# First batch's main keys turned with all 128 rows, a PSUM bank per head, and identity products in TensorE's planned gaps there

## The chip, the cores and the metric

One core of a Trainium2 chip. The metric is the device time of one execution in microseconds; a profiled execution has its own time, and its span runs from the first to the last instruction.

## The reference

Three layers, all in fp32, on 4 batches, 8 heads, 576 positions, head size 64. Attention: q and k are rotated by position, `scores = q·k / 8`, a softmax over the keys, then times v. The heads are put side by side to 512 columns. The first moe block mixes each position with the one before (`mu_k`, `mu_r`), computes `k = relu(xk @ w_k)`, `v = k*k @ w_v`, `r = sigmoid(xr @ w_r)`, and gives `r * v`. The second computes `h = relu(x @ w_in)`, normalises its second half over the columns, mixes it over the positions with `w_spatial`, multiplies it with the first half, and applies `w_out`.

## The kernel before, in words

The kernel has two halves. In the first one, attention for the batches runs beside the first moe block; in the second, the rest runs batch by batch. The change touches only the first half.

There the work is cut in 72 units of attention (`unit`, from line 305): 18 per batch, each 128 queries of a pair of heads; the last 64 queries of two neighbouring pairs make one unit together, the tail (every ninth unit has `tail` set). A unit does, in this order of need: `scores` (line 315; the first batch, `i < EXACT`, in plain fp32 with 64 rows for each head, line 338; later batches as three fp32r products, lines 327 and 330); `top`, the row maximum, on VectorE (line 342); `expo`, the exponential with its row sum, on ScalarE, one for each head (line 347); `total`, `norm` and `spread`, which make 1/sum and copy it to 64 columns (lines 351, 354, 358); `turn(0)` and `turn(1)`, which turn the probabilities so that the keys lie on the partitions (line 367); `turn_rest` for the last 64 keys and the spread sums (lines 377, 380, 381); `take(0)`, `take(1)` on ScalarE and `take_rest` on VectorE, which copy the turned blocks from PSUM to SBUF (lines 395, 400, 402); and for every second unit `values`, the product with v, (line 409) and `gather`, which scales it and writes it into the moe input (line 421).

`turn(n)` issues eight transposes: for each of four blocks of 128 keys of head n, two of 64 rows (queries 0 to 63 and 64 to 127). The result `t` has two PSUM banks, one for each half of the queries, so that each copy (`take`, four of the eight blocks of both banks) reads both banks.

`feed` (from line 461) holds the first moe block of a batch, `mk` (line 505) and `mv` (line 544), which runs beside the next batch's attention. `prep` (from line 236) loads and rotates q and k on VectorE (lines 249, 257), and `weight64` prepares weights on VectorE, ScalarE and GpSimd (lines 142 to 174). The identity `ident` is written once by GpSimd (lines 222 and 225).

All of this is put in order by a planner (`Plan`, lines 51 to 101). Each step has an engine, a planned duration, the steps it needs, a rank, and a slot that it takes or gives back. `order` plays the plan through: of the steps that are ready, an engine takes the one of least rank; TensorE takes one that is ready first, and pays `SWITCH` where the kind of its steps changes. The slots are PSUM banks: two `m` banks (values, remaining turns, moe), one `t` (the two banks of the turns). The steps are then emitted sorted by their planned beginning, and each engine runs its own in that order; the framework adds the waits. The planned costs that matter here: `turn` 0.27 us, `expo` 0.93, `top` 0.75, `take` 0.59.

Of the kernel before, what the change touches and what calls it, by code (L numbers as in the profile page):

```python
# [7 lines left out]
F32 = mybir.dt.float32  # L8
# [17 lines left out]
EXACT = NP  # L26
WB, GB, WB2, GB2 = 3, 2, 3, 2
RAW, ROT, VB, PFB, PTB, XTS = 2, 4, 2, 3, 2, 6
KB, RLB, VSB = 4, 2, 1
EARLY, EVERY = 24, 2.9  # L30
WAIT, SWITCH, BONUS = 0.3, 0.1, 0.0
SIDES = slice(0, HALF), slice(HALF, S)
HEAD = slice(0, 64), slice(64, 128)

# [16 lines left out]
class Plan:  # L51


    def __init__(self, room):
        self.steps, self.room = [], room

    def add(self, eng, us, fn, deps=(), rank=0.0, after=0.12, take=None, give=None, port=False, kind=None):
        s = Step(eng, us, fn, deps, rank, after, take, give, port, kind)
        self.steps.append(s)
        return s  # L60

    def order(self):
        free = dict.fromkeys(("PE", "ACT", "DVE", "POOL", "SP"), 0.0)
        room = {k: [(0.0, i) for i in range(n)] for k, n in self.room.items()}
        todo = {e: [s for s in self.steps if s.eng == e] for e in free}
        left, port, kind = len(self.steps), {"DVE": 0.0, "POOL": 0.0}, None
        while left:
            best = None
            for e, steps in todo.items():
                ready = []  # L70
                for s in steps:
                    if any(d.end is None for d in s.deps) or s.take and not room[s.take]:
                        continue
                    ready.append((max([free[e]] + [d.end + d.after for d in s.deps]
                                      + ([min(room[s.take])[0]] if s.take else [])
                                      + ([port["POOL" if e == "DVE" else "DVE"]] if s.port else [])), s))
                if ready:
                    soon = min(t for t, _ in ready) + (WAIT if e != "PE" else 0.0)
                    t, s = min((x for x in ready if x[0] <= soon), key=lambda x: (x[1].rank - (BONUS if e == "PE" and x[1].kind == kind else 0.0), x[0]))
                    if best is None or t < best[0]:  # L80
                        best = t, s
            t, s = best
            s.begin, s.end = t, t + s.us
            if s.eng == "PE" and s.kind != kind:
                kind = s.kind
                s.end += SWITCH
            free[s.eng] = s.end
            if s.port:
                port[s.eng] = s.end
            if s.take:  # L90
                s.slot = min(room[s.take])[1]
                room[s.take].remove(min(room[s.take]))
            if s.give:
                room[s.give.take].append((s.end + s.after, s.give.slot))
            todo[s.eng].remove(s)
            left -= 1
        return sorted(self.steps, key=lambda s: s.begin)

    def emit(self):
        for s in self.order():  # L100
# [4 lines left out]
def body(ctx: ExitStack, tc, qp, kp, vp, cs, mu_k, mu_r, w_k, w_v, w_r, w_in, w_sp, b_sp, w_out, out):  # L105
    nc = tc.nc
# [8 lines left out]
    ps_m = ph1p.enter_context(tc.tile_pool(name="ps_m", bufs=1, space=PSUM))  # L115
# [3 lines left out]
    ps_t = att.enter_context(tc.tile_pool(name="ps_t", bufs=1, space=PSUM, side="right"))  # L119
# [4 lines left out]
    v_dram = [dram.tile([128, 4, S], F32, tag=f"vd{b}", name=f"vd{b}") for b in range(B)]  # L124

    cst = at.tile([128, 2, S], F32, name="cst")
    ends = [[at.tile([128, 128], F32R, tag=f"qe{i}{k}", name=f"qe{i}{k}") for k in range(2)] for i in range(2)]
    ident = const.tile([128, 128], F32, name="ident")
    mix4 = const.tile([128, NP, 4], F32, name="mix4")
# [72 lines left out]
    wv = [wpool.tile([128, NFC, DM], F32R, tag=f"wB{i}", name=f"wv{i}") for i in range(2)]  # L202

    second, fed = {}, set()
    plan = Plan({"m": 2, "e": 4, "t": 1, "ww": WB, "wg": GB})
    add = plan.add

    def which(m):
# [3 lines left out]
    ropes, vloads, exps, turned, valued, xdone, stored = {}, {}, {}, {}, {}, {}, {}  # L212
# [92 lines left out]
    def unit(m):  # L305
        w = which(m)
        tail = len(w) == 2
        st = units[m] = {}
        g, k = divmod(m, 9)
        part = 0 if tail else (k - (k > 4)) % 2  # L310
# [49 lines left out]
        def turn(n, slot=None):  # L360

            if n == 0:
                st["t"] = ps_t.tile([128, 2, 8, 64], F32, tag="t", name=f"t{m}")
            for c in range(4):
                for h, r in enumerate(HEAD):
                    k = 64 * (h if tail else n) + 128 * c
                    nc.tensor.transpose(st["t"][:, h, 4 * n + c, :], st["p"][r, n, k:k + 128], ident[r, r])  # L367

        def turn_rest(slot):

            pt, p = ps_m.tile([128, 4, 128], F32, tag=f"m{slot}", name=f"u{m}"), st["p"]
            st["u"] = pt
            if tail:
                for u in range(2):
                    for k in range(2):
                        for j, r in enumerate(HEAD):
                            nc.tensor.matmul(pt[r, u, HEAD[k]], st["r"][r, u, :] if k else p[r, u, 512 - 512 * j:576 - 512 * j],  # L377
                                             ident[r, r], start=True, stop=True)
            else:
                nc.tensor.transpose(pt[:, 0, :], p.rearrange("p a b -> p (a b)")[:, 512:640], ident)  # L380
                nc.tensor.transpose(pt[:, 1, :], st["r"].rearrange("p a b -> p (a b)"), ident)

        def turned_to(u):
            d = into[u if tail else 0]
# [4 lines left out]
        def take(k):  # L389
            o = turned_to(k)  # L390
            if tail:
                o = o[:, 0:8, 256:320].rearrange("p (h c) q -> p h c q", h=2)
            else:
                o = o[:, 4 * k:4 * k + 4, 128 * part:128 * part + 128].rearrange("p c (h q) -> p h c q", h=2)
            nc.scalar.copy(o, st["t"][:, :, 4 * k:4 * k + 4, :])  # L395
# [39 lines left out]
        t = add("ACT", 0.2, total, [exps[m, 1]], m - 0.3)  # L435
        nm = add("DVE", 0.17, norm, [t], m - 0.3)
        sp = add("ACT", 0.26, spread, [nm], m - 0.3)
        late = [y for d in into for y in freed.get(d["n"] - PTB, [])]
        t = add("PE", 0.27, lambda slot: turn(0), [exps[m, 0]], m + -0.02, take="t", kind="s")
        turned[m, 0] = x = add("PE", 0.27, lambda: turn(1), [exps[m, 1], t], m + 0.05, kind="s")  # L440
        x = add("ACT", 0.59, lambda: take(1), [x] + late, m - 0.2, 0.05)
        x = add("ACT", 0.59, lambda: take(0), [x] + late, m - 0.2, give=t)
        turned[m, 1] = t = add("PE", 0.55 if tail else 0.22, turn_rest, [sp], m + 0.2, take="m", kind="t")
        y = add("DVE", 0.55 if tail else 0.42, take_rest, [t] + late, m - 0.2, give=t)
        for d in into:
            d["ev"] += [x, y]
        if part and k != 3 or tail:
            v = add("PE", 2.9 if duo["cols"] > 256 else 2.3, values, duo["ev"] + [vloads[w[0][0]]], m + 0.9, take="m", kind="v")
            i = w[0][0]
# [205 lines left out]
    for n, (k, c, q) in enumerate(todo):  # L655
        if k == "x":
            mix_steps(c, 76 + n, close)
        else:
            add("SP", 0.4, lambda k=k, c=c, q=q: nc.sync.dma_start(
                raw(second[k == "i"][:, :, c, DM * q:DM * q + DM]), w_dram[0 if k == "r" else 1 + q][:, c]), [close], 76 + n, 5)  # L660
    add("ACT", 1.3, opened, [close], 75)
    with tc.manual_schedule():
        plan.emit()

# [236 lines left out]
```

## Time and profile before

| | us |
|---|---|
| median of 3 runs | 772.25 |
| lowest, highest | 770.16, 772.73 |
| the profiled execution | 773.33 |
| its span | 771.5 |
| TensorE busy in the span | 723.5 |

Engines: PE is TensorE, PEld its weight loads, DVE is VectorE, ACT ScalarE, POOL GpSimd, SP SyncE. Busy shares of TensorE are of pipelined matmuls, whose ends are modelled. A plain fp32 matmul leaves two records. A granted clock of 1.00 is TensorE's full 2.4 GHz, 0.50 is 1.2 GHz.

### The profile page before, as it was taken

Reading aid. Unit: us, or ns where it says so; the run is one execution under the profiler, and the core shown is the slowest. Engines: PE = TensorE matmul, PEld = TensorE weight load, DVE = VectorE, ACT = ScalarE, POOL = GpSimd, SP = SyncE. Lnnn points to the kernel's source line nnn. Section 1 sums busy time; section 2 is a strip of 40 time slices with the busy share of each in tenths; the row PEclk is TensorE's granted clock in tenths of the full one; section 3 lists DMA queues with packets and bytes.
Section 4 is the critical chain, followed back from the end, with each engine's and each line's share of the span. In section 5 each row is a group of like instructions: output and inputs, shape, how many; then the busy total and the mean of one; then the engine's idle time right before and its main releaser. Section 6 shows DMA issues by size and latency. Waiting matters only on the chain.

```text
span 771.5 us, 15273 instructions
## 1 busy us (share of the span) xinstructions
PE 723.5 (94%) x6208; PEld 636.9 (83%) x6208; DVE 473.5 (61%) x881; ACT 456.4 (59%) x1045; POOL 112.5 (15%) x132
## 2 busy tenths in 40 slices
PE   3787779899999999999999999999999999999998
PEld 2554448698798788888798799989989999998997
DVE  5769898886886986886866444247363342545111
ACT  4667888887877887777887554246334332533211
POOL 2243245012002021022031000002020000101000
PEclk9989899999999999999999999999999999999999
DMA  8355432442543353443351085082201212010101
GB/s 296 117 158 167 132 116 79 149 122 87 177 132 135 119 173 107 134 143 105 119 174 63 16 297 192 25 264 83 62 1 63 63 47 78 17 31 1 62 1 62
DMA packets 35273, 84.20 MB, mean 109 GB/s; under 512 B 4545, under 2 KB 10433, under 8 KB 35202
## 3 DMA queue, kind: packets, MB, share of 16 engines
q1 hardware_dynamic: 34658, 82.63, 32.6%
q8 instruction: 49, 0.80, 0.4%
q10 hardware_dynamic: 544, 0.59, 0.3%
q14 instruction: 22, 0.18, 0.1%
HBM read 60.65 MB, written 22.55 MB: 108 GB/s over the span
## 4 chain that ended last, share of the span: by engine, by line
PE 87%; ACT 5%; DMA 4%; DVE 3%; issue 1%; SPq 1%; ACTq 0%; DVEq 0%
PE v L409 12%; PE mk L505 12%; PE mv L544 11%; PE sp L680 8%; PE r L680 7%; PE u L680 7%; PE hv L744 7%; PE o L680 7%; PE t L367 6%; PE s L330 5%; PE s L338 3%; ACT pt L395 3%; PE u L380 1%; PE s L327 1%; DMA I-6413_6414<-xd 1%; DMA wi<-wd 1%
## 5 line engine op out<-in xcount | busy, mean ns | idle before, releaser
L342 DVE TENSOR_REDUCE sm<-s 128x1 f32<-128x576 f32 x144 | 106.0, 750 | 28.4 <-PE s L330 20.3
L347 ACT ACTIVATE pf<-s,sm 128x576 f32<-128x576 f32 x144 | 106.6, 749 | 10.6 <-DVE sm L342 10.5
L505 PE MATMUL mk<-x,wk 128*128 128x288 f32 x768 | 110.8, 300 | 0.7 <-DVE pt L400 0.7
L544 PE MATMUL mv<-kh,wv 128*128 128x288 f32 x512 | 109.2, 299 | 0.9 <-DVE pt L402 0.5
L505 PEld LDWEIGHTS mk<-x,wk 128*128 128x128 f32 x768 | 104.0, 190 | 1.7 <-PE u L377 0.8
L395 ACT COPY pt<-t 128x512 f32<-128x512 f32 x144 | 77.6, 589 | 41.5 <-PE t L367 40.7
L409 PE MATMUL v<-pt,vt 128*64 128x256 f32 (+1 forms) x640 | 90.8, 433 | 8.5 <-ACT pt L395 8.2
L367 PEld LDWEIGHTS t<-ident,pf 64*128 64x128 f32 x1152 | 56.3, 141 | 47.0 <-ACT pf L347 22.6
L367 PE MATMUL t<-ident,pf 64*128 64x64 f32 x1152 | 68.8, 232 | 21.0 <-ACT pf L347 20.9
L544 PEld LDWEIGHTS mv<-kh,wv 128*128 128x128 f32 x512 | 83.8, 188 | 2.7 <-issue 1.2
L409 PEld LDWEIGHTS v<-pt,vt 128*64 128x64 f32 x640 | 45.7, 144 | 42.9 <-ACT pt L395 11.3
L544 PE MATMUL mv<-kl,wv 128*128 128x288 f32 x256 | 75.7, 296 | 0.4 <-DVE kl L523 0.4
L680 PE MATMUL sp<-ws,vn 128*128 128x288 f32 x384 | 53.9, 295 | 0.0
L680 PE MATMUL r<-xr,wr 128*128 128x288 f32 x384 | 52.5, 296 | 1.2 <-ACT vs L550 1.2
L680 PE MATMUL o<-g,wo 128*128 128x288 f32 x384 | 52.9, 296 | 0.5 <-ACT os L803 0.5
L680 PEld LDWEIGHTS r<-xr,wr 128*128 128x128 f32 x384 | 51.7, 188 | 1.8 <-ACT vs L550 1.5
L680 PEld LDWEIGHTS sp<-ws,vn 128*128 128x128 f32 x384 | 52.4, 188 | 0.7
L680 PEld LDWEIGHTS o<-g,wo 128*128 128x128 f32 x384 | 51.7, 188 | 1.4 <-ACT os L803 1.2
L680 PE MATMUL u<-x,wi 128*128 128x288 f32 x384 | 52.0, 296 | 0.0
L680 PEld LDWEIGHTS u<-x,wi 128*128 128x128 f32 x384 | 51.6, 188 | 0.3
L249 DVE TENSOR_TENSOR raw<-raw,cst 128x1152 f32<-128x1152 f32 (+1 forms) x34 | 46.7, 1380 | 5.8 <-DMA raw<-kp 5.3
L544 PEld LDWEIGHTS mv<-kl,wv 128*128 128x128 f32 x256 | 48.2, 188 | 0.6 <-DVE kl L523 0.6
(346 smaller groups left out, 1182.0 us busy)
## 6 DMA issues: line engine op xcount, KB each, us to landing
raw<-kp SPq DMA_DIRECT2D x15, 576.0 KB, 3.9
raw<-qp SPq DMA_DIRECT2D x15, 576.0 KB, 4.7
vt<-vp SPq DMA_DIRECT2D x16, 320.0 KB, 3.8
xd<-xt SPq DMA_DIRECT2D x16, 288.5 KB, 4.3
vd<-vs SPq DMA_DIRECT2D x32, 144.0 KB, 1.8
v<-vd SPq DMA_DIRECT2D x16, 288.0 KB, 2.8
out<-os SPq DMA_DIRECT2D x15, 288.0 KB, 2.1
wi<-wd SPq DMA_DIRECT2D x8, 512.0 KB, 9.1
```

Source lines behind the costliest of these rows:

```text
L249: nc.vector.tensor_tensor(t["raw", k][:, :, z], t["raw", k][:, :, z], cst[:, :, z], op=ALU.mult)
L330: nc.tensor.matmul(ps[j][:, h, :HALF], t[a, 0][r, 128 * c:128 * c + 128], t[b, 1][r, x], **f)
L338: nc.tensor.matmul(o, q[r, 128 * c:min(128 * c + 128, S)], k[r, h * HALF:(h + 1) * HALF], start=True, stop=True)
L342: nc.vector.tensor_reduce(st["sm"][:, 0, j:j + 1], st["s"][j][:, :, :HALF], axis=AX.XY, op=ALU.max, negate=True)
L347: nc.scalar.activation(st["p"][:, j, :].rearrange("p (a b) -> p a b", a=2), st["s"][j][:, :, :HALF], AF.Exp, bias=st["sm"][:, 0, j:j + 1], ...
L367: nc.tensor.transpose(st["t"][:, h, 4 * n + c, :], st["p"][r, n, k:k + 128], ident[r, r])
L395: nc.scalar.copy(o, st["t"][:, :, 4 * k:4 * k + 4, :])
L409: nc.tensor.matmul(pv[HEAD[j], z], v[:, 4 * j + c if c < 4 else 8 + j, :], pt[:, 4 * j + c if c < 4 else 8, z], start=c == 0, stop=c == 4)
L505: nc.tensor.matmul(ps[:, :HALF], wk[w][:, c, fc * 128:(fc + 1) * 128], a[:, c, :], start=k == 0, stop=k == 11)
L544: nc.tensor.matmul(xs["v", dc][:, :HALF], wv[w][:, fc, dc * 128:(dc + 1) * 128], a, start=k == 0, stop=k == 23)
L680: nc.tensor.matmul(ps[:, h, :HALF], w, a[:, h * HALF:(h + 1) * HALF], start=m == 0, stop=m == n - 1)
L744: nc.tensor.matmul(ps[:, :FS], x[a][:, d, c:c + 128], wi[w][:, d, FS:], start=k == 0, stop=k == 11)
```

## The change

For the units of the first batch, `turn`, `take` and their steps are replaced. `turn_whole(n)` turns head n (n = 0, 1) with four transposes of 128 rows into one bank, and its third call (n = 2) does what `turn_rest` did, into one of the same two banks; each of the three takes a `t` slot of its own, of which there are now two. `take_whole(n)` copies one bank. In a tail unit the four queries-by-keys blocks of each pair are turned one by one (eight for each n), and each bank is copied in two parts. Planned costs: 0.44 us for n = 0 and 1, 0.22 for the rest (0.5, 0.5 and 0.8 in a tail). The other batches keep their steps, under another slot name `d`, and wait once for all of the first batch's copies (`whole`), as both use the same two PSUM banks (`both_banks`).

The planner also gets a filler. Ahead of each TensorE step that it places before a planned 125 us, with an m bank free, it counts how many products of 0.22 us fit in TensorE's idle time less 0.3 us, at most 20, and puts that many in: `filler` multiplies the identity with itself (128 x 128 by 128 columns, fp32) into the m bank that is free the longest. Nothing reads the result.

```diff
--- before.py
+++ after.py
@@ -29,6 +29,7 @@
 KB, RLB, VSB = 4, 2, 1
 EARLY, EVERY = 24, 2.9
 WAIT, SWITCH, BONUS = 0.3, 0.1, 0.0
+FILL, FILL_US, FILL_MARGIN, FILL_MOST = 125.0, 0.22, 0.3, 20
 SIDES = slice(0, HALF), slice(HALF, S)
 HEAD = slice(0, 64), slice(64, 128)
 
@@ -52,7 +53,7 @@
 
 
     def __init__(self, room):
-        self.steps, self.room = [], room
+        self.steps, self.room, self.filler = [], room, None
 
     def add(self, eng, us, fn, deps=(), rank=0.0, after=0.12, take=None, give=None, port=False, kind=None):
         s = Step(eng, us, fn, deps, rank, after, take, give, port, kind)
@@ -63,7 +64,7 @@
         free = dict.fromkeys(("PE", "ACT", "DVE", "POOL", "SP"), 0.0)
         room = {k: [(0.0, i) for i in range(n)] for k, n in self.room.items()}
         todo = {e: [s for s in self.steps if s.eng == e] for e in free}
-        left, port, kind = len(self.steps), {"DVE": 0.0, "POOL": 0.0}, None
+        left, port, kind, fills = len(self.steps), {"DVE": 0.0, "POOL": 0.0}, None, []
         while left:
             best = None
             for e, steps in todo.items():
@@ -80,6 +81,14 @@
                     if best is None or t < best[0]:
                         best = t, s
             t, s = best
+            if s.eng == "PE" and self.filler and t < FILL and room["m"]:
+                slot = min(room["m"])
+                begin = max(free["PE"], slot[0])
+                n = min(int((t - begin - FILL_MARGIN) / FILL_US), FILL_MOST)
+                if n > 0:
+                    f = Step("PE", n * FILL_US, lambda n=n, slot=slot[1]: self.filler(n, slot), [], 0.0, 0.0, None, None, False, None)
+                    f.begin, f.end = begin, begin + f.us
+                    fills.append(f)
             s.begin, s.end = t, t + s.us
             if s.eng == "PE" and s.kind != kind:
                 kind = s.kind
@@ -94,7 +103,7 @@
                 room[s.give.take].append((s.end + s.after, s.give.slot))
             todo[s.eng].remove(s)
             left -= 1
-        return sorted(self.steps, key=lambda s: s.begin)
+        return sorted(self.steps + fills, key=lambda s: s.begin)
 
     def emit(self):
         for s in self.order():
@@ -124,6 +133,8 @@
     v_dram = [dram.tile([128, 4, S], F32, tag=f"vd{b}", name=f"vd{b}") for b in range(B)]
 
     cst = at.tile([128, 2, S], F32, name="cst")
+    both_banks = ps_t.tile([128, 2, 8, 64], F32, tag="t", name="both")
+    whole = []
     ends = [[at.tile([128, 128], F32R, tag=f"qe{i}{k}", name=f"qe{i}{k}") for k in range(2)] for i in range(2)]
     ident = const.tile([128, 128], F32, name="ident")
     mix4 = const.tile([128, NP, 4], F32, name="mix4")
@@ -202,7 +213,7 @@
     wv = [wpool.tile([128, NFC, DM], F32R, tag=f"wB{i}", name=f"wv{i}") for i in range(2)]
 
     second, fed = {}, set()
-    plan = Plan({"m": 2, "e": 4, "t": 1, "ww": WB, "wg": GB})
+    plan = Plan({"m": 2, "e": 4, "t": 2, "d": 1, "ww": WB, "wg": GB})
     add = plan.add
 
     def which(m):
@@ -368,8 +379,8 @@
 
         def turn_rest(slot):
 
-            pt, p = ps_m.tile([128, 4, 128], F32, tag=f"m{slot}", name=f"u{m}"), st["p"]
-            st["u"] = pt
+            p = st["p"]
+            pt = st["u"] = ps_m.tile([128, 4, 128], F32, tag=f"m{slot}", name=f"u{m}") if isinstance(slot, int) else slot
             if tail:
                 for u in range(2):
                     for k in range(2):
@@ -379,6 +390,31 @@
             else:
                 nc.tensor.transpose(pt[:, 0, :], p.rearrange("p a b -> p (a b)")[:, 512:640], ident)
                 nc.tensor.transpose(pt[:, 1, :], st["r"].rearrange("p a b -> p (a b)"), ident)
+
+        def turn_whole(n, slot):
+
+            pt = st["t", n] = both_banks[:, slot].rearrange("p a b -> p (a b)").rearrange("p (c q) -> p c q", c=4)
+            p = st["p"]
+            if tail and n < 2:
+                for u in range(2):
+                    for c in range(4):
+                        k = 64 * n + 128 * c
+                        nc.tensor.transpose(pt.rearrange("p c (h q) -> p (c h) q", h=2)[:, 4 * u + c, :],
+                                            p[HEAD[n], u, k:k + 128], ident[HEAD[n], HEAD[n]])
+            elif n < 2:
+                for c in range(4):
+                    k = 64 * n + 128 * c
+                    nc.tensor.transpose(pt[:, c, :], p[:, n, k:k + 128], ident)
+            else:
+                turn_rest(pt)
+
+        def take_whole(n):
+            x = st["t", n].rearrange("p c (h q) -> p (c h) q", h=2)
+            for u in range(len(into)):
+                if tail:
+                    nc.scalar.copy(turned_to(u)[:, 4 * n:4 * n + 4, 256:320], x[:, 4 * u:4 * u + 4, :])
+                else:
+                    nc.scalar.copy(turned_to(u)[:, 4 * n:4 * n + 4, 128 * part:128 * part + 128], st["t", n])
 
         def turned_to(u):
             d = into[u if tail else 0]
@@ -436,14 +472,28 @@
         nm = add("DVE", 0.17, norm, [t], m - 0.3)
         sp = add("ACT", 0.26, spread, [nm], m - 0.3)
         late = [y for d in into for y in freed.get(d["n"] - PTB, [])]
-        t = add("PE", 0.27, lambda slot: turn(0), [exps[m, 0]], m + -0.02, take="t", kind="s")
-        turned[m, 0] = x = add("PE", 0.27, lambda: turn(1), [exps[m, 1], t], m + 0.05, kind="s")
-        x = add("ACT", 0.59, lambda: take(1), [x] + late, m - 0.2, 0.05)
-        x = add("ACT", 0.59, lambda: take(0), [x] + late, m - 0.2, give=t)
-        turned[m, 1] = t = add("PE", 0.55 if tail else 0.22, turn_rest, [sp], m + 0.2, take="m", kind="t")
-        y = add("DVE", 0.55 if tail else 0.42, take_rest, [t] + late, m - 0.2, give=t)
-        for d in into:
-            d["ev"] += [x, y]
+        if w[0][0] < EXACT:
+            ready = [[exps[m, 0], exps[m, 1]] if tail else [exps[m, 0]], [exps[m, 1]], [sp]]
+            xs = []
+            for n in range(3):
+                turned[m, n] = t = add("PE", (0.5, 0.5, 0.8)[n] if tail else (0.44, 0.44, 0.22)[n], lambda slot, n=n: turn_whole(n, slot),
+                                       ready[n], m + 0.1 * n, take="t", kind="t")
+                if n < 2:
+                    xs.append(add("ACT", 0.68 if tail else 0.59, lambda n=n: take_whole(n), [t] + late, m - 0.2, give=t))
+                else:
+                    xs.append(add("DVE", 0.55 if tail else 0.42, take_rest, [t] + late, m - 0.2, give=t))
+            whole.extend(xs)
+            for d in into:
+                d["ev"] += xs
+        else:
+            t = add("PE", 0.27, lambda slot: turn(0), [exps[m, 0]] + whole, m + -0.02, take="d", kind="s")
+            turned[m, 0] = x = add("PE", 0.27, lambda: turn(1), [exps[m, 1], t], m + 0.05, kind="s")
+            x = add("ACT", 0.59, lambda: take(1), [x] + late, m - 0.2, 0.05)
+            x = add("ACT", 0.59, lambda: take(0), [x] + late, m - 0.2, give=t)
+            turned[m, 1] = t = add("PE", 0.55 if tail else 0.22, turn_rest, [sp], m + 0.2, take="m", kind="t")
+            y = add("DVE", 0.55 if tail else 0.42, take_rest, [t] + late, m - 0.2, give=t)
+            for d in into:
+                d["ev"] += [x, y]
         if part and k != 3 or tail:
             v = add("PE", 2.9 if duo["cols"] > 256 else 2.3, values, duo["ev"] + [vloads[w[0][0]]], m + 0.9, take="m", kind="v")
             i = w[0][0]
@@ -659,6 +709,14 @@
             add("SP", 0.4, lambda k=k, c=c, q=q: nc.sync.dma_start(
                 raw(second[k == "i"][:, :, c, DM * q:DM * q + DM]), w_dram[0 if k == "r" else 1 + q][:, c]), [close], 76 + n, 5)
     add("ACT", 1.3, opened, [close], 75)
+
+    def filler(n, slot):
+
+        ps = ps_m.tile([128, 512], F32, tag=f"m{slot}", name=nc.get_next_instruction_name())
+        for _ in range(n):
+            nc.tensor.matmul(ps[:, :128], ident, ident, start=True, stop=True)
+
+    plan.filler = filler
     with tc.manual_schedule():
         plan.emit()
 
```

## Rows read from the trace of the kernel before

**Rows 1.** The page: the span, and the granted clock in 40 slices.

```profile
span 771.5 us, 15273 instructions
...
PEclk9989899999999999999999999999999999999999
```

**Rows 2.** Busy time by stretches: stretch, length, us (x instructions) per engine, PEclk, DMA.

```profile
8.20:27.30 19.10, 14.94 (x80) 10.10 (x80) 15.27 (x26) 10.81 (x26) 5.05 (x4) 1.00 0.67 229
...
37.80:44.80 7.00, 6.54 (x44) 3.76 (x42) 4.88 (x9) 4.76 (x12) 5.15 (x3) 0.53 0.36 104
44.80:85.70 40.90, 29.80 (x302) 19.35 (x299) 35.07 (x66) 32.16 (x79) 12.28 (x12) 1.00 0.48 148
85.70:92.10 6.40, 6.28 (x39) 3.55 (x39) 5.58 (x11) 4.87 (x13) 2.28 (x2) 0.50 0.55 188
...
8.20:111.70 103.50, 79.63 (x684) 50.95 (x684) 86.46 (x159) 75.79 (x187) 35.24 (x27) 0.93 0.48 154
111.70:771.50 659.80, 643.84 (x5526) 585.97 (x5524) 384.62 (x719) 379.13 (x857) 75.87 (x92) 1.00 0.30 100
```

The engines stand in the order PE, PEld, DVE, ACT, POOL.

**Rows 3.** The chain that ended last, 0 to 140 us: start, us, what.

```profile
8.22 2.54 PE s L338 x8
...
22.86 4.53 PE v L409 x20
...
27.79 1.03 PE s L338 x8
...
61.55 0.98 ACT pt L395 x2
...
62.57 2.38 PE v L409 x20
...
66.37 0.24 PE t L367 x8
66.61 0.26 PE u L380
66.87 0.12 PE u L381
...
116.05 3.11 PE mk L505 x12
...
120.94 1.59 PE mk L505 x12
```

**Rows 4.** TensorE in order of time, first turns of units: start, us, line, [idle before].

```profile
12.51 0.69 PE L367 MATMUL t<-ident,pf 64*128 64x64 f32 x8 [1.80 <-ACT pf L347]
...
18.27 0.69 PE L367 MATMUL t<-ident,pf 64*128 64x64 f32 x8 [1.79 <-ACT pf L347]
...
27.33 0.47 PE L367 MATMUL t<-ident,pf 64*128 64x64 f32 x8
...
36.32 0.46 PE L367 MATMUL t<-ident,pf 64*128 64x64 f32 x8 [1.53 <-ACT pf L347]
...
45.49 0.47 PE L367 MATMUL t<-ident,pf 64*128 64x64 f32 x8
...
69.03 0.47 PE L367 MATMUL t<-ident,pf 64*128 64x64 f32 x8 [2.05 <-ACT pf L347]
...
74.70 0.47 PE L367 MATMUL t<-ident,pf 64*128 64x64 f32 x8
...
78.33 0.46 PE L367 MATMUL t<-ident,pf 64*128 64x64 f32 x8 [1.53 <-ACT pf L347]
```

**Rows 5.** Weight loads, 45 to 85 us, by form: busy us, mean ns.

```profile
L380 PEld LDWEIGHTS u<-ident,pf 128*128 128x128 f32 x8 | 1.1, 138 | 0.5
```

**Rows 6.** TensorE's waits, 8 to 116 us: total us, times, longest.

```profile
PE t L367 <- ACT pf L347: 20.9, 12, 2.1
...
PE v L409 <- ACT pt L395: 4.0, 6, 0.8
```

**Rows 7.** All engines in order of time: the identity's last instruction.

```profile
1.63 0.28 POOL L225 TENSOR_SCALAR_AFFINE_SELECT ident<-ident 128x128 f32<-128x128 f32 x1
```

## The prediction

> **What bounds the kernel now.** I read the page first, for where TensorE is not at its full clock [rows 1]: in the row PEclk only the third and the fifth of the forty slices, between 39 and 96 us, hold an 8; everything later is at full speed. So I cut the span in stretches [rows 2]. From 111.7 us to the end TensorE is busy for 643.8 of 659.8 us: that stretch is a queue of TensorE work, and whatever ends earlier ahead of it ends the kernel earlier by about as much. From 8.2 to 111.7 us, the first batch's eighteen units, TensorE is busy for only 79.6 of 103.5 us, VectorE for 86.5, ScalarE for 75.8. Nothing is full there; the units are a chain from engine to engine, with VectorE nearest to being the bound.
>
> Two of those stretches have a granted clock near 0.5, the lower level of 1.2 GHz (the rows from 37.8 and from 85.7) [rows 2]. A third is not marked: until 27.3 us the clock column says 1.00, but the same instructions take twice as long as later, eight score records 2.54 us against 1.03, twenty value records 4.53 against 2.38 [rows 3]. So the array ran at 1.2 GHz from its first matmul to 27.3 us too. A short fourth stretch is the first moe product, 3.11 us for twelve records against 1.59 for the next twelve [rows 3]. What TensorE did before the fall is the same each time: a wait of over 1.5 us ahead of a unit's first turn, and turns beside it. Before each rise it ran value products or moe products back to back.
>
> What that costs is read from the pace, since a lost TensorE microsecond need not be a lost chain microsecond. From one unit's first turn to the next unit's [rows 4], at full clock a step without value products takes 3.63 us (74.70 to 78.33) and one with them 5.67 (69.03 to 74.70), 6.2 if these have 320 columns (some 0.5 us more). The steps in the low stretches take 5.76 (12.51 to 18.27), 9.06 (18.27 to 27.33) and 9.17 (36.32 to 45.49); one more like the last lies in the stretch from 85.7.
>
> **The change, part by part.**
>
> *The clock.* If the products in the gaps hold the clock, the steps lose 5.76 − 3.63 = 2.1, 9.06 − 5.67 = 3.4, 9.17 − 6.2 = 3.0, and about 2.7 for the fourth: 11.2 us. To that come 1.5 us of the first scores and 1.5 of the first moe product [rows 3]: 14.2 us. VectorE will not give all of it: it has 86.5 us of work in 103.5 us [rows 2]. In its densest long stretch, 44.8 to 85.7 us, it is busy for 35.1 of 40.9 us, 86%, and at 92% the 86.5 us would need 94 us. So 9.5 us is the most that I allow up to 111.7 us, and 11 with the moe product. I take three quarters of that, **−8.5 us**, because planned gaps are not the real ones and the clock may still fall once or twice. Ends: 0, if the products do not hold it, and −14.2.
>
> *The turns.* Before, each unit had sixteen turns of 64 rows in two blocks of eight; now eight of 128 rows in two blocks of four. A block of eight takes 0.24 us behind scores [rows 3]. A 128-row turn is in the trace as line 380 and line 381: 0.26 us for the first behind other shapes, 0.12 for the one after it [rows 3]. Four in a row are 0.26 + 3 × 0.12 = 0.62 us, that is 0.38 more per block. The first block's extra lies under the second head's exponential, which the scores behind it wait for anyway; without that cover it would be another 0.38 per unit. The second block's lies on the path to the copy: at worst 18 × 0.38 = 6.8 us. Against it stands the bank per head: both copies waited for both blocks and took 0.98 us together [rows 3]; now the first head's copy can run while scores and the second block run, so value products and the next exponential wait for one copy, 0.5 us less. At twelve or so places of the chain that is −6 us at best. The remaining turns move from the m banks to the same two banks; they wait only for the first head's copy, and the moe side gains room in m. Ends −6 and +6.8; nothing says which side wins, and part of either is covered by VectorE. I take **0**.
>
> The Trainium skill (TensorEngine Tiling, Key Properties) says that a change of tiling mode drains TensorE. The new turns stand between 64-row scores, so by it each unit has some two changes more; the rows agree as far as 0.26 against 0.12 goes, and by that 0.14 us the turns alone would cost up to 5 us. That is inside the upper end above.
>
> *The products in the gaps.* A plain fp32 matmul leaves two records (four score matmuls are eight records), so an identity product of 128 columns is about two of the 0.12 us records: 0.24 us, where the planner counts 0.22. The other end is a weight load that nothing hides: 0.138 us more per record [rows 5], 0.52 us per product. I take 0.24, because the pair 380/381, which loads 128 × 128 weights for each record too, already shows 0.12 from end to end. TensorE waits 20.9 us at twelve places for the exponential and 4.0 us at six places for the copy [rows 6]. If the planned gaps are like these, a gap of 1.75 us gets (1.75 − 0.3) / 0.22 = 6 products and one of 0.67 us gets 1: some 80 in all. Six take 1.44 us, which ends ahead of the wait's end. The planner's exponential (0.93 us) is a little longer than the real one, so some gaps are overfilled: 0.05 us at some twenty places, **+1 us**. Ends: 0, and 12 × (6 × 0.52 − 1.75) = 16 us.
>
> *The block ahead of the first scores.* There the planned gap is some 6 us (the planner lets the second load of line 246 land 3.9 us after its issue at 0.8, and two rotations of 1.2 us follow), so the cap of 20 products holds. They need the identity, which is written at 1.63 + 0.28 = 1.9 us [rows 7]; the first scores start at 8.22 [rows 3]. At the low clock twenty would take 20 × 0.48 = 9.6 us and end at 11.5, 3.3 us late. The value run at 22.86 was slow nearly to its end, 4.5 us on, so I take half of the twenty as slow: 10 × 0.48 + 10 × 0.24 = 7.2 us, to 9.1. **+1 us**, between 0 and +3.3; the scores themselves are then quick, which is counted above.
>
> *The rest.* Later batches keep their turns; they only wait once for the last copies of the first batch (a planned order, no cost). VectorE's copies and ScalarE's amount of work stay. No DMA is added or moved on purpose, but the planner draws the whole order anew, which I hold to be worth ±2 us.
>
> **Sum.** 773.3 (the profiled execution: its span of 771.5 and 1.8 around it) − 8.5 + 0 + 1 + 1 = 766.8. The median of the three runs is 772.25, so 1.1 below the execution that the durations come from; I say **766 us**, 0.8% less than the median. This measurement can tell a change from none from about 0.3%, 2.3 us.
>
> **The rivals.**
>
> *VectorE keeps the pace (0.17).* If VectorE can be no denser than the 86% of 44.8 to 85.7 us [rows 2], the first batch needs 86.5 / 0.857 = 100.9 us and gains 2.6, with the moe product 4; less the 2 of the fills: 773.3 − 4 + 2 = 771.3. For it: VectorE is the fullest engine there. Against it: some of its work is weight preparation for later, which can slide behind 111.7 us.
>
> *The products outlast the gaps (0.15), the slower side.* Place: the twelve waits for the exponential. If a product costs 0.45 us, six take 2.7 us in gaps of 1.75: +0.95 × 12 = 11.4 in place of the +1, which gives 777.2. It decides from where the twelve overruns eat the 7.5 us that the rest leaves: 0.63 us per gap, a product of about 0.4 us. For it: two 128-column loads per product, at 0.138 us each. Against it: line 381 directly behind 380.
>
> *The clock does not follow (0.10).* The low stretches came after waits and turns, and the turns stay. Without the 8.5 and with the fills still to pay, 773.3 + 2 = 775.3, and less if the copies gain. Against it: between 44.8 and 85.7 us the clock held over waits up to 2 us. The Trainium skill (TensorE: Matmul & The Clock Gate, Part 4) says that the full clock does not engage for transposes; by it the new turns would bring nothing and the identity products alone would have to hold the clock. The trace before shows no transposes without matmuls beside them, so it does not test that.
>
> *All of it (0.06).* The clock held throughout and the copies gaining half of their 6 us: 773.3 − 14.2 − 3 + 2 = 758.1.
>
> **How the numbers follow.** The forecast has 0.52, its own range 761.5 to 770. 758 to 776 takes in the fastest case and leaves out most of the slower one and the far ends. Faster by over 0.3% (under 770): nearly all of the forecast, 0.5, a third of the first rival and the last: 0.62. Slower (over 774.6): the second rival and some 0.04 of the third, 0.19. The rest, 0.19, is within.
>
> **What would show it.** Right: from 8 to 120 us no stretch with a granted clock near 0.5, the first value products near 2.4 us instead of 4.53, TensorE busy for over 90% there, the eighteenth unit's turns done some 6 to 8 us earlier, VectorE over 90% busy. The turn block: four records in 0.6 us, with one copy starting before the second block. Wrong: products that end later than the exponential's end in many gaps, first scores starting after 10 us, clock rows at 0.5 as before, or the first batch ending earlier with the gain lost behind 112 us.

## The result, and the profile after

The changed kernel takes **776.6 us** (median; 776.09 to 776.89), the one before 772.3 beside it: ratio 1.0062, 95% interval 1.0041 to 1.0084. It is slower, and outside the range that was given. The profiled execution took 776.09 us, its span 774.3. The page, beside [rows 1]:

```profile
span 774.3 us, 15525 instructions
...
PEclk9999999999999999999999999999999999999999
```

The clock column never falls. The stretches of [rows 2] say the same (columns as there):

```profile
8.20:27.30 19.10, 17.16 (x131) 12.66 (x130) 15.78 (x27) 11.63 (x28) 3.60 (x4) 1.00 0.66 217
8.20:111.70 103.50, 96.60 (x734) 70.22 (x733) 82.40 (x150) 74.11 (x183) 31.89 (x26) 1.00 0.47 152
111.70:774.30 662.60, 648.17 (x5570) 589.25 (x5570) 388.29 (x728) 382.64 (x865) 77.74 (x94) 1.00 0.30 100
```

TensorE is busy for 96.6 of the 103.5 us, where it was 79.6, and yet less was done: VectorE, which was near to being the bound, has 82.4 us of its work behind it at 111.7 us in place of 86.5 [rows 2]. Where the time went is read from the chain, beside [rows 3, 4]:

```profile
1.97 7.56 PE I-120_121 L717 x40
9.54 0.69 PE s L349 x4
...
11.33 2.43 PE I-184_185 L717 x20
13.75 0.44 PE both L407 x4
14.19 1.17 PE s L349 x8
15.36 0.59 PE both L407 x4
...
23.19 2.38 PE v L445 x20
...
46.22 0.58 ACT pt L417
46.80 0.74 ACT pf L358 x2
...
47.59 0.66 PE both L407 x4
...
79.58 0.66 PE both L407 x4
...
114.83 0.39 PE t L378 x8
```

Four score records take 0.69 us in place of 1.27 (half of the 2.54 of eight), the twenty value records 2.38 in place of 4.53 [rows 3]. But unit 18 turns for the first time at 114.76 in TensorE's order of time (the chain counts it from 114.83), in the kernel before at 111.73. From there to the end it is 774.3 − 114.76 = 659.5 us here and 771.5 − 111.73 = 659.8 before: all that was lost was lost in the first batch. Cut at the first turns of units 0, 6, 12 and 18, all in TensorE's order of time (13.59, 47.59, 79.58, 114.76 here; before 12.51 and 78.33 [rows 4], 111.73, and 49.13 for unit 6):

| us | to unit 0 | 0 to 6 | 6 to 12 | 12 to 18 | unit 18 turns at |
|---|---|---|---|---|---|
| before | 12.51 | 36.62 | 29.20 | 33.40 | 111.73 |
| after | 13.59 | 34.00 | 31.99 | 35.18 | 114.76 |

Units 6 to 12 ran at full clock in both kernels, and there the changed one needs 2.8 us more. So something other than the clock is worse. The waits of the changed kernel from 8 to 112 us (engine, tile and line, releaser: us in total, times, longest):

```profile
ACT pf L358 <- DVE sm L353: 14.5, 12, 8.6
...
DVE pt L438 <- ACT pt L417: 9.6, 11, 1.2
ACT pt L417 <- PE both L392: 8.5, 12, 1.4
...
ACT pt L417 <- PE both L407: 2.1, 5, 0.7
```

Line 417 is the copy of one head's bank. In twelve of its waits it is released not by its own turns (line 407) but by line 392, the remaining turns, which write the other bank. And VectorE's copy of the remaining turns (line 438) waits 9.6 us for ScalarE's copy. One place in the timeline (start, duration, what; the idle time before it and its releaser in brackets):

```profile
45.31 0.66 PE L407 MATMUL both<-ident,pf 128*128 128x128 f32 x4
...
45.91 0.27 PE L392 MATMUL both<-ident,rb 128*128 128x128 f32 x1
...
46.22 0.58 ACT L417 COPY pt<-both 128x512 f32<-128x512 f32 x1 [0.90 <-PE both L392]
46.70 0.75 ACT L358 ACTIVATE pf<-s,sm 128x576 f32<-128x576 f32 x1
46.84 0.42 DVE L438 COPY pt<-both 128x256 f32<-128x256 f32 x1 [0.67 <-ACT pt L417]
...
47.18 0.75 DVE L353 TENSOR_REDUCE sm<-s 128x1 f32<-128x576 f32 x1
...
47.59 0.66 PE L407 MATMUL both<-ident,pf 128*128 128x128 f32 x4
...
47.96 0.74 ACT L358 ACTIVATE pf<-s,sm 128x576 f32<-128x576 f32 x1 [0.42 <-DVE sm L353]
```

The users of the two banks stand in a row: turns, remaining turns, ScalarE's copy, VectorE's copy, and behind VectorE's copy the row maximum for which the next exponential waits. In the kernel before, the remaining turns had a tile of their own, and the two copies lay beside each other:

```profile
57.11 1.07 ACT L395 COPY pt<-t 128x512 f32<-128x512 f32 x2 [0.52 <-PE t L367]
...
57.53 0.41 DVE L402 COPY pt<-u 128x256 f32<-128x256 f32 x1
```

### The profile page after: what moved, and what is told of

It reads as the page before. It is cut to its first block, busy times and chain, and to the rows that moved or that the text cites. A ratio compares the mean times of both kernels' runs of the same rounds, so it can differ in the third digit from the quotient of the medians.

```text
span 774.3 us, 15525 instructions
## 1 busy us (share of the span) xinstructions
PE 751.0 (97%) x6332; PEld 665.7 (86%) x6332; DVE 473.0 (61%) x881; ACT 458.2 (59%) x1049; POOL 111.0 (14%) x132
## 4 chain that ended last, share of the span: by engine, by line
PE 87%; ACT 5%; DVE 4%; DMA 3%; issue 1%; SPq 1%; POOL 0%; ACTq 0%; DVEq 0%; POOLq 0%
PE mv L594 11%; PE mk L555 11%; PE v L445 10%; PE sp L738 8%; PE r L738 7%; PE u L738 7%; PE hv L802 7%; PE o L738 6%; PE s L341 5%; PE t L378 4%; PE s L349 3%; PE both L407 2%; PE s L338 1%; PE u L391 1%; DMA I-6434_6435<-xd 1%; ACT pf L358 1%
## 5 line engine op out<-in xcount | busy, mean ns | idle before, releaser
L445 PE MATMUL v<-pt,vt 128*64 128x256 f32 (+1 forms) x640 | 86.4, 411 | 4.6 <-ACT pt L431 4.1
L431 ACT COPY pt<-t 128x512 f32<-128x512 f32 x108 | 58.3, 589 | 27.9 <-PE t L378 27.5
L378 PEld LDWEIGHTS t<-ident,pf 64*128 64x128 f32 x864 | 38.9, 138 | 16.0 <-issue 6.2
L260 DVE TENSOR_TENSOR raw<-raw,cst 128x1152 f32<-128x1152 f32 (+1 forms) x34 | 45.1, 1330 | 5.9 <-DMA raw<-kp 5.4
L378 PE MATMUL t<-ident,pf 64*128 64x64 f32 x864 | 47.9, 229 | 0.1
```

Source lines behind the costliest of these rows:

```text
L260: nc.vector.tensor_tensor(t["raw", k][:, :, z], t["raw", k][:, :, z], cst[:, :, z], op=ALU.mult)
L445: nc.tensor.matmul(pv[HEAD[j], z], v[:, 4 * j + c if c < 4 else 8 + j, :], pt[:, 4 * j + c if c < 4 else 8, z], start=c == 0, stop=c == 4)
```

## The experiments

The **first theory**: the tile `both`, one tile of two banks, ties its users together, although they use different banks; the clock is as good as predicted, and the tie costs more than it gives. The **rivals**: the products are late and push the chain, or the 128-row turns themselves cost it. Each kernel was timed beside the kernel before (medians 772.62, 773.27 and 772.44 in the three groups of runs). All figures of medians and ratios stand in the table at the end of this section.

**The products alone, with the old turns.** The kernel before with the filler, as in the change.

```diff
+FILL, FILL_US, FILL_MARGIN, FILL_MOST = 125.0, 0.22, 0.3, 20
...
+    plan.filler = filler
```

> The kernel before with the products in the planned gaps alone; turns, copies and their order stay as before. Theory A (the products hold the clock, and what the change lost it lost at the turns): granted clock 0.99 or more with no stretch near 0.5 after 10 us, the low steps of 9 us back to about 6, unit 18's first turn near 103 us instead of 111.7, time 761 to 766. Theory B (64-row turns let the clock fall whatever stands in the gaps, only the 128-row turns hold it): stretches near 0.5 remain, 770 to 774. Theory C (the products themselves delay the chain): clock held but 774 or more.

772.2 us, no difference from before. None of the three theories came out whole: the clock held in the first batch, as theory A had it, but the time lies in the range of theory B, which had denied that. Unit 18 does turn at 108.38, 3.4 us earlier, but 2.2 of them are lost behind it (770.4 − 108.38 = 662.0 us to the end, before 659.8): from 120 to 140 us, where the products have stopped, the clock is 0.93:

```profile
120.00:140.00 20.00, 18.30 (x186) 15.34 (x184) 16.73 (x30) 17.00 (x43) 8.80 (x7) 0.93 0.10 31
```

And 3.4 is little beside the full clock's worth. The chain shows why (start, duration, what):

```profile
32.72 1.79 PE I-460_461 L676 x16
34.50 0.40 PE t L377 x8
34.90 0.42 PE I-490_491 L676 x2
35.32 1.17 PE s L348 x8
```

The products run right up to the turns, and one more product (two records) stands between the turns and the scores: TensorE no longer waits for the exponential, the exponential's result waits for TensorE. The products also make their neighbours longer: eight 64-row turns take 0.40 us behind them and 0.24 behind scores [rows 3], eight score records 1.17 and 1.03 [rows 3]. That is about 0.15 us for each change between instructions of 128 and of 64 rows.

**The whole turns without the products.** The changed kernel, its order unchanged, nothing put in the gaps.

```diff
-    plan.filler = filler
+    plan.filler = None
```

> The changed kernel without its products; same order of everything else. Theory A (products hold the clock): low stretches come back, some 20 us at 0.5 in the middle and a slow start to 27 us, time 780 to 788. Theory B (the 128-row turns hold the clock alone): clock as in the changed kernel, time within 1.5 us of its 776.6. Theory C (products delay the chain): faster, under 773.

785.9 us. The profiled execution was the quickest of seven (780.32), so its stretches are rather too good:

```profile
8.20:27.30 19.10, 15.21 (x64) 8.33 (x64) 14.01 (x23) 10.61 (x26) 3.53 (x3) 0.82 0.58 200
8.20:111.70 103.50, 82.36 (x514) 48.60 (x514) 78.53 (x144) 70.72 (x174) 30.88 (x25) 0.93 0.44 146
```

This is theory A's range, and low stretches are back. The clock column reads 0.93 in the first batch, as before the change [rows 2], but the two figures can't be compared as they stand: the column counts the kernel before as 1.00 until 27.3 us, while its records ran at half pace there [rows 3]. With those 19.1 us counted at 0.5 its mean is about 0.84; here the unmarked slow start ends at about 16 us (the second head's turns at 15.58 still take 0.98), and the mean is about 0.89 (both are estimates from the rows). So unit 18 turns at 118.56, 6.8 us later than before, at a higher clock: the new turns as they were built cost at least those 6.8 us.

**Two tiles in place of one.** The same order, the same products, the same two banks; each bank is now a tile of its own. (The later batches' turns then need a pool of their own, opened at their first turn.)

```diff
-    both_banks = ps_t.tile([128, 2, 8, 64], F32, tag="t", name="both")
+    both_banks = [ps_w.tile([128, 8, 64], F32, tag=f"w{i}", name=f"bank{i}") for i in range(2)]
...
-            pt = st["t", n] = both_banks[:, slot].rearrange("p a b -> p (a b)").rearrange("p (c q) -> p c q", c=4)
+            pt = st["t", n] = both_banks[slot].rearrange("p a b -> p (a b)").rearrange("p (c q) -> p c q", c=4)
```

> The changed kernel with the two banks of the first batch's turns as two tiles instead of one; same order, same products. Theory A1 (the framework waits by the tile, so the second head's copy waits for the remaining turns in the other bank, 0.23 us, and VectorE's copy for ScalarE's, 0.6 us, which puts off the maximum and the next exponential): those waits vanish, steps without value products fall from 4.0 to about 3.6 us, 768 to 771. Theory A2 (the longer turns on TensorE, 0.59 us per block against 0.24, make the loss by themselves): 774 to 776.6.

768.2 us, 8.4 less than with one tile, and within the range of theory A1, though a step without value products fell only from 4.10 to 3.82 us (unit 7 to 8), not to 3.6 (unit 18 turns 9.3 us earlier; 2.0 are lost behind it, where the clock of 120 to 140 us is 0.91). The waits from 8 to 112 us, and the same place of the timeline:

```profile
ACT pf L359 <- DVE sm L354: 9.6, 4, 8.3
ACT pt L421 <- PE bank L411: 9.3, 18, 1.2
...
DVE pt L442 <- PE bank L396: 1.8, 4, 0.9
```

```profile
42.40 0.66 PE L411 MATMUL bank<-ident,pf 128*128 128x128 f32 x4
...
43.00 0.27 PE L396 MATMUL bank<-ident,rb 128*128 128x128 f32 x1
...
43.09 0.59 ACT L421 COPY pt<-bank 128x512 f32<-128x512 f32 x1 [0.68 <-PE bank L411]
...
43.31 0.42 DVE L442 COPY pt<-bank 128x256 f32<-128x256 f32 x1
43.58 0.75 ACT L359 ACTIVATE pf<-s,sm 128x576 f32<-128x576 f32 x1
43.65 0.75 DVE L354 TENSOR_REDUCE sm<-s 128x1 f32<-128x576 f32 x1
...
44.44 0.74 ACT L359 ACTIVATE pf<-s,sm 128x576 f32<-128x576 f32 x1
```

ScalarE's copy starts 0.69 us after its turns began (43.09 − 42.40), where it was 0.91; VectorE's 0.91, where it was 1.53; the maximum 1.25, where it was 1.87; the next exponential but one 2.04, where it was 2.65. VectorE waits for ScalarE's copy no more, and the copies overlap; ScalarE's copy still waits 9.3 us in all, but for its own turns. Most of the 0.6 us is thus VectorE's wait for the other copy, the smaller part (0.2) ScalarE's for the remaining turns.

**Two tiles without the products.** As above, with `plan.filler = None`.

> Two tiles and no products. With A and A1: low stretches as without products, and the waits gone: 773 to 780. With B (128-row turns hold the clock): 767 to 771, like the two-tile kernel with products.

767.5 us: the products as placed by the change bring nothing here. The range of the theories that let the low stretches come back (773 to 780) was missed, that of theory B, in which the 128-row turns hold the clock, was met. The clock held rather well without products (0.97 in the column, about 0.94, an estimate, with an unmarked slow start to about 15 us):

```profile
8.20:111.70 103.50, 86.27 (x607) 55.20 (x607) 90.17 (x164) 81.42 (x200) 32.45 (x26) 0.97 0.49 163
```

In TensorE's order of time, the first turns, the second head's turns and the first value products:

```profile
12.30 1.09 PE L411 MATMUL bank<-ident,pf 128*128 128x128 f32 x4 [1.80 <-ACT pf L359]
...
15.49 0.66 PE L411 MATMUL bank<-ident,pf 128*128 128x128 f32 x4
...
21.82 2.60 PE L449 MATMUL v<-pt,vt 128*64 128x256 f32 x20
```

The turns are at full pace from 15.49 us on, without any product, and the first value records take 2.60 us in place of 4.53 [rows 3]. Unit 18 turns at 106.59, 5.1 us before the kernel before; 4.9 of them are gained between units 0 and 6 (31.75 us, before 36.62), where that kernel ran slowly. So with the whole turns and nothing added the clock is faster here, and it holds until about 80 us. Whether the turns themselves raise it, or what stands around them, these kernels do not separate.

**Two tiles, products ahead of the first scores only.** `FILL` 7.0 and `FILL_MOST` 12.

> Two tiles, and of the products only one block of 12 ahead of the first scores. If a warm array is worth something to the first units and a block that ends by 8 us costs nothing: first scores start at 8.0 to 8.3 us at full clock, unit 18's first turn at 104 to 106 us (106.6 without products, 105.5 with all), 764 to 767. Rival (the clock falls again in the waits that follow, or ScalarE and VectorE set the pace of the first units anyway): unit 18 at 106.5 or later, time within 1.5 us of the two-tile kernel without products, 767.5.

768.7 us, above the 764 to 767 that was expected and within 1.5 us of the kernel without products, as the rival said. The first scores are quick, but the clock falls soon after (0.84 and 0.94):

```profile
8.20:30.00 21.80, 16.23 (x94) 9.86 (x96) 18.62 (x32) 14.44 (x35) 5.50 (x5) 0.84 0.71 234
30.00:60.00 30.00, 25.31 (x182) 16.34 (x180) 25.44 (x46) 22.51 (x56) 13.00 (x10) 0.94 0.51 163
```

One block at the start does not hold it over what follows.

**Fewer products, in three kernels.** The planner leaves 0.9 us of each gap free, not 0.3, and puts in at most 12: with two tiles, with the old turns, and with the shared tile as in the change.

```diff
-FILL, FILL_US, FILL_MARGIN, FILL_MOST = 125.0, 0.22, 0.3, 20
+FILL, FILL_US, FILL_MARGIN, FILL_MOST = 125.0, 0.22, 0.9, 12
```

> Two tiles, products with a margin of 0.9 us in place of 0.3 and at most 12 in a block. If the products of the two-tile kernel cost what they gain because they end late (first scores at 9.2 in place of 8.0 us, blocks ending at the same time as or behind the exponential): 764 to 767. Rival (the products are simply not needed with 128-row turns and cost nothing either): 767 to 769.

> The kernel before with products, margin 0.9 us and at most 12 in a block. If late products ate the gain of the held clock in the kernel with old turns (772.2): 766 to 769 with the clock still at 0.99 or more. Rival (the gaps that are left let the clock fall as before): 771 to 773, stretches near 0.5 between 30 and 95 us.

> The changed kernel, one tile as it is, with a margin of 0.9 us and at most 12 products in a block. If its loss has two parts, the one tile (8.4 us by the two-tile kernel) and late products, this takes away the second alone: 773 to 775.5, 1 to 3 us under its 776.6, as the margin did with two tiles (768.2 to 766.6). Rival (the late products are most of the loss, as with old turns, where the margin gave 7.5 us): 768 to 770.

766.6, 764.7 and 777.9 us. With the old turns the smaller dose (more room and a lower cap together) is worth 7.5 us (772.2 to 764.7), more than was expected, and this kernel beats both of the case. The stretch and its waits for the exponential (where the kernel before had 20.9 us in twelve waits [rows 6]):

```profile
8.20:111.70 103.50, 91.86 (x918) 67.39 (x914) 92.72 (x175) 83.64 (x206) 39.63 (x31) 1.00 0.54 179
```

```profile
PE t L377 <- ACT pf L357: 4.8, 11, 0.6
...
PE v L419 <- ACT pt L405: 4.1, 7, 0.7
```

With two tiles the medians differ by 1.5 us (768.2 and 766.6), but the two were not run beside each other and their intervals overlap, so that gain is not shown. Beside the old turns with the same dose, in the same group of runs, two tiles are 1.9 us slower (766.6 against 764.7). With the shared tile the expectation was a **miss**: it was to gain some us and gained none. Its ties stayed (`DVE pt L438 <- ACT pt L417` again 9.1 us in eleven waits), and the clock was 0.98 in the first batch: what the lighter dose saved was given back there.

**Only the remaining turns moved away.** The two heads still share one tile; the remaining turns go back to an m bank.

```diff
-                                       ready[n], m + 0.1 * n, take="t", kind="t")
+                                       ready[n], m + 0.1 * n, take="t" if n < 2 else "m", kind="t")
```

> The changed kernel with the remaining turns back in an m bank, a tile of its own, and the two heads still in the one two-bank tile. If the loss comes from the remaining turns sharing the tile with the second head (its copy waits for them, VectorE's copy waits for ScalarE's): both waits gone, 768 to 771. Rival (the two heads' own sharing, copy of the one against turns of the other, is the loss): 774 to 777.

777.5 us, but the edit was incomplete: the planner gave an m slot, and the turns still wrote into the shared tile, over turned values that were still to be copied. It tells nothing of the question. With the m bank's own tile really used:

```diff
+            if n == 2:
+                return turn_rest(slot)
```

> The changed kernel with the remaining turns in an m bank, a tile of its own, this time with their step using that bank; the two heads still in the one two-bank tile, margin 0.3. If the loss comes from the remaining turns sharing the tile (the second head's copy waits for them on TensorE, VectorE's copy for ScalarE's): both waits gone, 768 to 771. Rival (the two heads' own sharing is the loss): 774 to 777.

768.7 us, and the waits are those of two tiles (the planner draws the order anew here, as the slots differ):

```profile
ACT pt L417 <- PE both L409: 9.7, 17, 1.2
ACT pf L358 <- DVE sm L353: 9.7, 4, 8.4
...
DVE pt L438 <- PE u L392: 2.1, 5, 1.0
```

So it is the remaining turns in the heads' tile that cost; that the two heads share one costs nothing that can be seen.

**The best one a little longer.** The old turns with the lighter dose, `FILL` 150 in place of 125.

> The kernel before with products, margin 0.9 us, at most 12 in a block, and products up to a planned 150 us in place of 125. If the fall of the clock that some kernels show between 130 and 140 us is worth filling for: 1 to 2 us under the kernel with 125 (764.7). Rival (the m banks are busy with the moe there and the gaps taken by its steps): within 1 us of it.

763.5 us. The two were not run beside each other, and their intervals overlap, so no difference between them is shown.

| kernel | us | ratio to before (95%) | unit 18 turns at |
|---|---|---|---|
| old turns, products | 772.2 | 1.0009 (0.9989 to 1.0029) | 108.38 |
| whole turns, no products | 785.9 | 1.0173 (1.0144 to 1.0203) | 118.56 |
| two tiles, products | 768.2 | 0.9949 (0.9931 to 0.9967) | 105.48 |
| two tiles, no products | 767.5 | 0.9935 (0.9914 to 0.9955) | 106.59 |
| two tiles, first block only | 768.7 | 0.9944 (0.9921 to 0.9967) | 105.72 |
| two tiles, fewer products | 766.6 | 0.9917 (0.9891 to 0.9944) | 103.04 |
| old turns, fewer products | 764.7 | 0.9891 (0.9864 to 0.9917) | 102.40 |
| shared tile, fewer products | 777.9 | 1.0059 (1.0040 to 1.0078) | 114.17 |
| remaining turns, incomplete edit | 777.5 | 1.0056 (1.0032 to 1.0080) | |
| remaining turns in an m bank | 768.7 | 0.9953 (0.9935 to 0.9972) | 106.02 |
| old turns, fewer products, to 150 | 763.5 | 0.9881 (0.9863 to 0.9899) | 102.88 |

## Why the prediction was wrong

*What bounds the kernel* was right: the time behind 111.7 us is a queue of TensorE work that neither kernel changed (659.8 and 659.5 us), and unit 18's first turn stands for the end.

*The clock, −8.5.* Right in kind and size for the products (three quarters of 11 are 8.25, so it was rounded up). With the old turns and the lighter dose unit 18 comes 9.33 us earlier (111.73 to 102.40), against a cap of 9.5: 0.8 of it ahead of unit 0, 5.8 between units 0 and 6, nothing from 6 to 12, 2.7 from 12 to 18, where 2.7 was written for the fourth low step. VectorE is then busy for 92.7 of 103.5 us, 90%, near the 92% of the cap. But the prediction gave all of this gain to the products; the whole turns in two tiles bring 5.1 us of it without any, and the two do not add up: with the lighter dose unit 18 turns at 103.04 with both and at 102.40 with the old turns.

*The turns, 0.* **This is the step that failed**: it counted waits by bank, in the sentences that the value products and the next exponential "wait for one copy, 0.5 us less" and that the remaining turns "wait only for the first head's copy". The first head's copy does run under the scores, as was said (at 49.02 us, beside scores from 48.40 to 50.08). But in the changed kernel the users of one tile wait on each other across its banks: the second head's copy for the remaining turns (8.5 us in twelve waits), and VectorE's copy for ScalarE's (9.6 us in eleven). The term was **+8.4 us** (768.2 to 776.6), above its upper end of +6.8, by a cause that was not in it.

The net of 0 for the turns themselves was right at full clock: with two tiles units 6 to 12 take 29.24 us with and 29.03 without products, before 29.20. A block of four takes 0.59 us on the chain, 0.62 was written. The Trainium skill (TensorEngine Tiling, Key Properties) says that a change of tiling mode drains TensorE. The trace agrees, near the 0.14 us that was taken from 0.26 against 0.12: in the chain under the result a block of four takes 0.44 us behind products of its own 128 rows and 0.59 behind 64-row scores, and the scores behind it 1.17 us, where behind 64-row turns they take 1.03 [rows 3]. In the pace of units 6 to 12 nothing of this shows, so something gained as much; the copy that runs early may be it, which no run separates.

*The products, +1 and +1.* A product in a run takes 2.43 / 10 = 0.243 us, 0.24 was written. The block ahead of the first scores took 7.56 us, 7.2 was written, and the scores started 1.3 us later (9.54, before 8.22 [rows 3]). But the two terms were too small for the dose of the change: with the old turns a room of 0.3 and a cap of 20 cost 772.2 − 764.7 = 7.5 us more than 0.9 and 12, at a full clock in the first batch in both. Unit 18 turns 6.0 us later (108.38 against 102.40), 1.7 of them already at unit 0 (13.39 against 11.69), behind the block ahead of the scores; what is left of the 7.5 is the clock's fall behind the first batch. The prediction let a product run late only where the planned exponential is too long, and counted changes of mode for the turns alone. In the trace products also stand between turns and scores, where a lone one takes 0.42 us and makes the scores 0.14 us longer.

*The sum.* Two tiles with the products, 768.2 us, is what the forecast described, 2.2 above its 766. The sharing adds 8.4. That the two are so close is in part luck: without products the same two tiles take 767.5 us, so on net the products add nothing there, where −8.5 + 1 + 1 was written; the gain is there with the whole turns alone, which were written as 0.

*The rivals.* The slower one (products that outlast the gaps, 777.2) comes near the number, but by another mechanism: its price of 0.45 us per product did not come in a run of products (0.243), and fewer products did not help the shared tile. VectorE did not keep the pace at 86%: it reached 90% with the old turns and the lighter dose. The clock followed, so "the clock does not follow" was wrong. It stood on a page: by the Trainium skill (TensorE: Matmul & The Clock Gate, Part 4) the full clock does not engage for transposes. For turns that stand between scores and value products the runs speak against what the prediction drew from it, that the new turns would bring nothing: with whole turns in two tiles and no product, TensorE was at full pace from 15.49 us to about 80, in the kernel before from 27.3 to 37.8. A stretch of transposes alone is in no run. What holds the clock is left open beyond that: products with 0.3 us of room held it at 1.00 while they lasted, with 0.9 us at 0.98 to 1.00; one block at the start did not hold it, and the fall at 120 to 140 us came in some kernels (0.93 with the old turns and 0.3 us of room) and not in others (1.00 with 0.9 us), behind the same wait of 1.5 us ahead of a tail's remaining turns.

## What to carry to other kernels

Before two engines are sent to different banks of one PSUM tile, look at what the waits name: here they followed the tile, and splitting one declaration in two, in the same order of work, was worth 8.4 us. Idle products that hold the clock must be late nowhere: leave room for the planner's error in each gap, since the gain (9.3 us at unit 18) was eaten with 0.3 us of room and up to 20 products, and kept with 0.9 and up to 12. Before a mean of the clock column is compared between kernels, like records must be compared too: a slow start can read 1.00. And a change of two parts is best split: the products alone, with room, make 764.7 us of 773, the new turns alone, in two tiles, 767.5, and both together, 766.6, are no better than the first.

## What was not expected

- A reader of one bank waited for a reader of the other: VectorE's copy for ScalarE's, eleven times, 9.6 us in all, and not once with two tiles. That this is by the tile is shown; why one reader waits for another is not.
- The heads' copies, which are two users of one tile too, cost nothing that shows when only the remaining turns have their own (768.7 against 768.2 us).
- The whole turns without products cost 9.2 us more than with them in the shared tile (785.9 against 776.6), and nothing in two tiles (767.5 against 768.2). That would fit if the tie made the waits in which the clock falls, and so cost twice; no run shows that the waits are the cause.
